# Zero matmuls ahead of the first data, transposes spread between score slots, and fewer, larger visits to attention

The kernel runs on one core of a Trainium2 chip. The metric is the device time of one execution in microseconds (us). Times are medians over several runs. In the traces PE is TensorE, which does the matmuls, DVE the vector engine and ACT the activation engine; PSUM is the memory that matmuls write and the other engines empty ("evacuate"). The *granted clock* is the share of full speed that the trace records for TensorE.

## The reference, cut to what matters

```python
# q, k, v: (8 batches, 12 heads, 448, 64); w_in: (768, 2048); w_out: (2048, 768)
scores = (q @ k.T) / sqrt(64)
attn   = maximum(scores, 0) ** 2 / 448
x      = (attn @ v), heads joined          # 3584 tokens x 768
h      = x @ w_in                          # "m1" below
g      = h * sigmoid(1.702 * h)
out    = g @ w_out                         # "m2" below
```

## The kernel before

A *unit* is four heads of one batch: 3 units a batch, 24 in all. A unit has 7 score *slots* of four 64x64 matmuls, which run in the four quadrants of the array at once. ACT takes the relu of a slot out of PSUM (`rl`), DVE squares it (`at`). After its 7 slots comes attn @ v (`av`, 28 matmuls), which DVE copies into `xt`, the input of m1. Scores and `av` share three PSUM tiles of two banks; m1 (`ht`), m2 (`op`) and the transposes (`tr`) share two tiles of one bank.

```python
def scores(u, j):                      # one slot
    sc = ps_s.tile([128, 2, 512], F32, tag="sc")        # ps_s: 3 buffers
    for s in range(2):
        for a in range(2):
            nc.tensor.matmul(out=sc[c, a, 0:S], lhsT=st["kT"][r, j, c], rhs=st["qT"][r, :, c], ...)

def trans_pe(u, n, cut):               # 14 transposes of q or k, then the copy
    ps = ps_m.tile([128, 1024], F16, tag="mm")           # ps_m: 2 buffers
    ...
    if cut:     nc.scalar.activation(out=t[:, 0:cut, :], in_=ps[:, 0:cut * 128], func=AF.Copy)
    if cut < J: nc.vector.tensor_copy(out=t[:, cut:J, :], in_=ps[:, cut * 128:J * 128])

# (cut)
# first stage: units 0 to 2, attention alone
trans_pe(0, "k", J); trans_pe(0, "q", 4)
while pos[0] < b0:
    visit(1); n += 1
    if n == 4:  trans_pe(1, "k", 0); trans_pe(1, "q", 0); ...   # also at 11 and 19
visit(3)
# second stage: first pass of m1 with units 3 to 5 between
for f in range(NF):
    m1(0, f)
    if f in (2, 8): trans_pe(4 + f // 8, "k", 0); trans_pe(4 + f // 8, "q", 0)
    if f % 2 == 1 or f > 12: visit(min(3, b1 - pos[0]))
prefetch(8, 0)
for m in range(gblk[0] // 2): m2(0, m, 0)
# third stage: m1 and m2 mixed; a visit of three slots whenever enough work has passed
#   (2.6 us at first, 4.2 us later)
```

From unit 6 on q and k are transposed by DMA: loaded, cast on DVE and GpSimd, then transposed. `visit(3)` issues three slots (or two slots and an `av`), and holds back the relu of the third until after the next m1 or m2.

## Time and profile before

| | before |
|---|---|
| time, median of the runs (range) | 407.58 us (407.47 to 409.45) |
| first score matmul | 8.31 us |
| first m1 matmul; its fifth, the first that needs unit 2 | 31.02; 32.15 us |
| first m2 matmul | 64.04 us |
| first visit after it | 77.81 us |
| end of the span in the profile | 406.5 us |

These are starts of instructions in the trace, counted from the span's start. They cut the run into stages. The page, the windows, the chain and the timeline of this kernel are shown in the prediction below. A window's row reads: from:to, length, busy time of PE, weight loads, DVE, ACT, GpSimd, then granted clock, DMA share and GB/s. A timeline row reads: start, length, engine, line, instruction, and in brackets the idle time before it with what ended it.

### The profile page before, as it was taken

Reading aid. Unit: us, or ns where it says so; the run is one execution under the profiler, and the core shown is the slowest. Engines: PE = TensorE matmul, PEld = TensorE weight load, DVE = VectorE, ACT = ScalarE, POOL = GpSimd, SP = SyncE. Lnnn points to the kernel's source line nnn. Section 1 sums busy time; section 2 is a strip of 40 time slices with the busy share of each in tenths; the row PEclk is TensorE's granted clock in tenths of the full one; section 3 lists DMA queues with packets and bytes.
Section 4 is the critical chain, followed back from the end, with each engine's and each line's share of the span. In section 5 each row is a group of like instructions: output and inputs, shape, how many; then the busy total and the mean of one; then the engine's idle time right before and its main releaser. Section 6 shows DMA issues by size and latency. Waiting matters only on the chain.

```text
span 406.5 us, 7792 instructions
## 1 busy us (share of the span) xinstructions
PE 383.3 (94%) x3192; PEld 202.2 (50%) x3192; DVE 190.7 (47%) x294; ACT 205.3 (51%) x297; POOL 130.8 (32%) x200
## 2 busy tenths in 40 slices
PE   3777899899999999999999999999999999999995
PEld 2433455344455455444455555444455555455564
DVE  0894763267746565564466455546354321010121
ACT  4984771576866454556475446546745511322100
POOL 8453424434433143244133324312311222323100
PEclk9989999999999999999999999999999999999999
DMA  8999997589775653955747396845121111111133
GB/s 122 194 204 205 205 290 153 115 192 246 184 173 111 165 139 72 261 106 134 183 70 166 71 198 153 197 51 82 40 52 35 39 40 40 40 39 40 39 79 78
DMA packets 65220, 50.85 MB, mean 125 GB/s; under 512 B 35744, under 2 KB 61728, under 8 KB 65184
## 3 DMA queue, kind: packets, MB, share of 16 engines
q1 hardware_dynamic: 47792, 35.60, 35.5%
q0 software_dynamic: 17152, 14.55, 24.0%
q8 instruction: 25, 0.41, 0.4%
q10 hardware_dynamic: 240, 0.20, 0.2%
q14 instruction: 11, 0.09, 0.1%
HBM read 45.61 MB, written 11.01 MB: 139 GB/s over the span
## 4 chain that ended last, share of the span: by engine, by line
PE 84%; DVE 6%; ACT 5%; issue 2%; DMA 2%; POOL 0%; ACTq 0%; DVEq 0%; POOLq 0%
PE op L278 35%; PE ht L249 33%; PE sc L144 7%; PE av L169 7%; ACT rl L158 4%; DVE at L159 3%; DMA q<-in_q_dram 1%; DVE rl L155 1%; DVE xt L186 1%; DMA qT<-q 1%; ACT gf L254 1%; DVE kT L134 1%; DVE k L101 0%; POOL gt L256 0%; PE tr L127 0%
## 5 line engine op out<-in xcount | busy, mean ns | idle before, releaser
L158 ACT ACTIVATE rl<-sc 128x896 f16<-128x896 f32 x165 | 144.8, 920 | 49.7 <-PE sc L144 49.7
L249 PE MATMUL ht<-xt,win 128*128 128x384 f16 (+1 forms) x768 | 158.4, 353 | 4.4 <-DVE kT L134 3.4
L159 DVE TENSOR_TENSOR at<-rl 128x896 f16<-128x896 f16 x168 | 114.9, 692 | 87.7 <-ACT rl L158 87.4
L256 POOL TENSOR_SCALAR gt<-gf 128x384 f16<-128x384 f32 (+1 forms) x128 | 77.6, 606 | 235.7 <-ACT gf L254 234.7
L278 PE MATMUL op<-wout,gt 128*128 128x384 f16 (+1 forms) x912 | 153.2, 323 | 0.0
L254 ACT ACTIVATE gf<-ht 128x384 f32<-128x384 f32 (+1 forms) x128 | 70.4, 550 | 119.6 <-PE ht L249 106.8
L278 PEld LDWEIGHTS <-gt 128*128 128x128 f16 x912 | 88.0, 98 | 60.5 <-issue 2.7
L249 PEld LDWEIGHTS <-win 128*128 128x128 f16 x768 | 71.1, 98 | 81.6 <-issue 21.4
L284 DVE TENSOR_SCALAR osb<-op 128x384 f32<-128x384 f32 (+1 forms) x57 | 31.3, 549 | 108.0 <-PE op L278 106.5
L144 PE MATMUL sc<-qT,kT 64*64 64x448 f16 x672 | 48.6, 367 | 6.8 <-DVE qT L134 3.0
L169 PE MATMUL av<-at,v 64*64 64x448 f16 x672 | 38.0, 360 | 2.3 <-ACT rl L158 1.4
L144 PEld LDWEIGHTS <-kT 64*64 64x64 f16 x672 | 17.5, 107 | 33.2 <-issue 22.9
L186 DVE CAST xt<-av 128x768 f16<-128x768 f32 (+2 forms) x36 | 26.9, 774 | 8.4 <-PE av L169 8.3
L169 PEld LDWEIGHTS <-v 64*64 64x64 f16 x672 | 20.1, 109 | 16.9 <-issue 7.1
L88 POOL DMA_DIRECT2D v<-in_v_dram x24 | 17.9, 745 | 5.2 <-DMA win<-in_moe_w_in_dram 2.9
L101 POOL CAST q<-qst 128x896 f16<-128x896 f32 x18 | 16.9, 941 | 0.3
L101 DVE CAST k<-kst 128x896 f16<-128x896 f32 x18 | 14.0, 785 | 0.0
L127 PE MATMUL tr<-ident,k 128*64 128x128 f16 x84 | 4.2, 253 | 5.2 <-DMA k<-in_k_dram 5.2
L134 DVE COPY qT<-tr 128x896 f16<-128x896 f16 (+1 forms) x6 | 3.4, 572 | 7.0 <-ACT qT L132 7.0
L127 PEld LDWEIGHTS <-k 128*64 128x64 f16 x84 | 3.1, 128 | 6.9 <-DMA k<-in_k_dram 5.2
L296 POOL DMA_DIRECT2D win<-in_moe_w_in_dram x8 | 5.4, 674 | 2.3 <-DMA q<-in_q_dram 1.3
L116 POOL DMA_DIRECT2D q<-in_q_dram x6 | 4.3, 713 | 3.0 <-PE sc L144 1.3
(17 smaller groups left out, 26.2 us busy)
## 6 DMA issues: line engine op xcount, KB each, us to landing
out_dram<-osb SPq DMA_DIRECT2D x54, 192.0 KB, 2.7
kst<-in_k_dram SPq DMA_DIRECT2D x18, 448.0 KB, 4.9
qst<-in_q_dram SPq DMA_DIRECT2D x18, 448.0 KB, 5.6
v<-in_v_dram POOLq DMA_DIRECT2D x24, 224.0 KB, 4.7
win<-in_moe_w_in_dram POOLq DMA_DIRECT2D x8, 384.0 KB, 11.5
wout<-in_moe_w_out_dram POOLq DMA_DIRECT2D x4, 768.0 KB, 12.1
k<-in_k_dram POOLq DMA_DIRECT2D x6, 224.0 KB, 8.9
q<-in_q_dram POOLq DMA_DIRECT2D x6, 224.0 KB, 8.9
```

The costliest lines, as they stand in the source:

```text
L88: nc.gpsimd.dma_start(out=x, in_=quad(v, b, pr))
L101: eng.tensor_copy(out=o, in_=i)
L144: nc.tensor.matmul(out=sc[c, a, 0:S], lhsT=st["kT"][r, j, c], rhs=st["qT"][r, :, c], start=True, stop=True)
L158: nc.scalar.activation(out=rl, in_=sc[:, :, 0:S], func=AF.Relu)
L159: nc.vector.tensor_tensor(out=at, in0=rl, in1=rl, op=ALU.mult)
L169: nc.tensor.matmul(out=st["av"][64 * a:64 * a + 64, s, 0:S], lhsT=st["v16"][r, a, 64 * j:64 * j + 64], rhs=at[r, a, :], start=(j == 0), st ...
L186: nc.vector.tensor_copy(out=xts[g][:, 2 * pr:2 * pr + 2, 64 * (lo - gcum[g]):64 * (hi - gcum[g])], in_=av[:, :, 64 * (lo - b * J):64 * (hi ...
L249: nc.tensor.matmul(out=ht[:, 0:n], lhsT=w[:, kk, fo:fo + 128], rhs=xts[g][:, kk, 0:n], start=(kk == 0), stop=(kk == NK - 1))
L254: nc.scalar.activation(out=gf[:, 0:n], in_=ht[:, 0:n], func=AF.Gelu_apprx_sigmoid, scale=1.0 / SC)
L256: nc.gpsimd.tensor_scalar(out=gts[g][:, f, 0:n], in0=gf[:, 0:n], scalar1=SC, scalar2=1.0, op0=ALU.mult, op1=ALU.mult)
L278: nc.tensor.matmul(out=op[:, 0:w], lhsT=gts[g][:, f, m * 128:(m + 1) * 128], rhs=wout[h][f // WO][:, f % WO, part * w:(part + 1) * w], sta ...
L284: nc.vector.tensor_scalar(out=ot[:, lo:lo + w], in0=op[:, 0:w], scalar1=1.0 / SC, scalar2=None, op0=ALU.mult)
```

## The change

The intent is to take away waits of TensorE in the first 100 us, and the cost of switching between full-array and quadrant work later. It has five parts.

```diff
+        nc.vector.memset(zero, 0.0)                      # 1: zero matmuls
+        zp = ps_m.tile([128, 512], F32, name="zp", tag="mm")
+        for _ in range(8):
+            nc.tensor.matmul(out=zp, lhsT=zero[:, 0:128], rhs=zero, start=True, stop=True)
...
-        if n == 4: trans_pe(1, "k", 0); trans_pe(1, "q", 0) ...
+        early = {("s", 0, 0): (1, "k"), ("s", 0, 1): (1, "q"), ("s", 1, 0): (2, "k"),   # 2: first stage
+                 ("s", 1, 1): (2, "q"), ("s", 2, 3): (3, "k"), ("s", 2, 5): (3, "q")}
+        # the transpose goes between a slot's matmuls and its relu; its copy is all on DVE
...
-            if f in (2, 8): trans_pe(4 + f // 8, "k", 0); trans_pe(4 + f // 8, "q", 0)
+        trans_at = {0: (4, "k"), 2: (4, "q"), 6: (5, "k"), 8: (5, "q")}                  # 3: m1 pass
...
+        prefetch(9, 7)                                   # 4: earlier prefetch
         for m in range(gblk[0] // 2):
             m2(0, m, 0)
+            if m == 0:
+                prefetch(9, 8)
...
+    for u in range(2 * NP, NU):                          # 5: visits
+        new = [("s", u, j) for j in range(J)]
+        if u > 2 * NP:
+            new.insert((1, 3, 2)[u % 3], ("v", u - 1, 0))
+        rest += new
+        n = 4 if rest[1][0] == "v" else 3                # slot, av, slot, slot - or three slots
...
-                moe.append((x, 4.2))
+                moe.append((x, 4.8))
```

The thresholds follow the number of visits (2.6 to 2.9, 4.2 to 4.8), and `at` gets an eleventh buffer.

More of the change, by code (lines that the diff above doesn't have):

```diff
@@ L52 @@
     rlp = ctx.enter_context(tc.tile_pool(name="rlp", bufs=3))
-    atp = ctx.enter_context(tc.tile_pool(name="atp", bufs=10))
+    atp = ctx.enter_context(tc.tile_pool(name="atp", bufs=11))
     xtp = ctx.enter_context(tc.tile_pool(name="xtp", bufs=3))
@@ L63 @@
     warm = cst.tile([1, 1], F32, name="warm")
+    zero = cst.tile([128, 512], F16, name="zero")
     win = [cst.tile([128, NK, WQ * 128], F16, name=f"win{i}") for i in range(NF // WQ)]
@@ L119, in load16, with trans_pe @@
         st[n + "16"] = x
-    def trans_pe(u, n, cut):
+    def trans_pe(u, n):
         st = units[u]
@@ L130, in trans_pe @@
         t = qkT.tile([128, J, 128], F16, name=f"{n}T", tag=f"{n}T")
-        if cut:
-            nc.scalar.activation(out=t[:, 0:cut, :], in_=ps[:, 0:cut * 128], func=AF.Copy)
-        if cut < J:
-            nc.vector.tensor_copy(out=t[:, cut:J, :], in_=ps[:, cut * 128:J * 128])
+        nc.vector.tensor_copy(out=t, in_=ps[:, 0:J * 128])
         st[n + "T"] = t
@@ L194 @@
     items = []
-    for u in range(NU):
-        late = u > 0 and u != 2 * NP
+    for u in range(2 * NP):
         items += [("s", u, 0), ("s", u, 1)]
-        if late:
+        if u:
             items.append(("v", u - 1, 0))
         items += [("s", u, j) for j in range(2, J)]
-        if u == 2 * NP - 1 or u == NU - 1:
-            items.append(("v", u, 0))
+    items.append(("v", 2 * NP - 1, 0))
+    rest = []
+    for u in range(2 * NP, NU):
[3 more added lines that the diff above has]
+        rest += new
+    visits = []
+    while rest:
+        n = 4 if rest[1][0] == "v" else 3
+        visits.append(rest[:n])
+        rest = rest[n:]
+    visits.append([("v", NU - 1, 0)])
     ats = {}
@@ L236, in visit, with visit4 @@
                 ats[u, j] = relu2(u, j, sc)
+    def visit4(new):
+        release()
+        if len(new) < 4:
+            items[:] = new
+            pos[0] = 0
+            return visit(3)
+        (_, u0, j0), (_, uv, _), (_, u1, j1), (_, u2, j2) = new
+        sc = scores(u0, j0)
+        ats[u0, j0] = relu2(u0, j0, sc)
+        for jj in range(J):
+            av_mm(uv, jj, ats.pop((uv, jj)))
+        sc1 = scores(u1, j1)
+        sc2 = scores(u2, j2)
+        xt_evac(uv)
+        done_units[0] = uv + 1
+        ats[u1, j1] = relu2(u1, j1, sc1)
+        held.append((u2, j2, sc2))
     gts = {}
@@ L344, with slot @@
         w1(1)
-        trans_pe(0, "k", J)
-        trans_pe(0, "q", 4)
+        trans_pe(0, "k")
+        trans_pe(0, "q")
         b0 = items.index(("s", NP, 0))
-        n = 0
-        while pos[0] < b0:
-            visit(1)
-            n += 1
-            if n == 4:
-                trans_pe(1, "k", 0)
-                trans_pe(1, "q", 0)
-                load16(4, "k")
-                load16(4, "q")
-                load_v(4)
-                w1(2)
-            if n == 11:
-                trans_pe(2, "k", 0)
-                trans_pe(2, "q", 0)
-                load16(5, "k")
-                load16(5, "q")
-                load_v(5)
-            if n == 19:
-                trans_pe(3, "k", 0)
-                trans_pe(3, "q", 0)
-                w1(3)
+        def slot(tr=None):
+            t, u, j = items[pos[0]]
+            pos[0] += 1
+            if t == "v":
+                for jj in range(J):
+                    av_mm(u, jj, ats.pop((u, jj)))
+                xt_evac(u)
+                return
+            sc = scores(u, j)
+            if tr:
+                trans_pe(*tr)
+            ats[u, j] = relu2(u, j, sc)
+        early = {("s", 0, 0): (1, "k"), ("s", 0, 1): (1, "q"), ("s", 1, 0): (2, "k"),
+                 ("s", 1, 1): (2, "q"), ("s", 2, 3): (3, "k"), ("s", 2, 5): (3, "q")}
+        loads = {("s", 0, 3): lambda: (load16(4, "k"), load16(4, "q"), load_v(4), w1(2)),
+                 ("s", 1, 3): lambda: (load16(5, "k"), load16(5, "q"), load_v(5)),
+                 ("s", 2, 4): lambda: w1(3)}
+        while pos[0] < b0:
+            it = items[pos[0]]
+            slot(early.get(it))
+            if it in loads:
+                loads[it]()
         visit(3)
-        b1 = items.index(("s", 2 * NP, 0))
+        b1 = len(items)
         pool_work = {1: lambda: w2(0, 0), 2: lambda: w2(0, 1),
                      4: lambda: w2(1, 0), 5: lambda: w2(1, 1)}
+        trans_at = {0: (4, "k"), 2: (4, "q"), 6: (5, "k"), 8: (5, "q")}
         for f in range(NF):
             m1(0, f)
-            if f in (2, 8):
-                trans_pe(4 + f // 8, "k", 0)
-                trans_pe(4 + f // 8, "q", 0)
+            if f in trans_at:
+                trans_pe(*trans_at[f])
             if f in pool_work:
@@ L402, with step_visit @@
         prefetch(8, 0)
+        prefetch(9, 7)
         for m in range(gblk[0] // 2):
             m2(0, m, 0)
-        def step_visit(n):
-            visit(n)
-            if pos[0] < len(items):
-                u = items[pos[0]][1] + (items[pos[0]][0] == "v")
+            if m == 0:
+                prefetch(9, 8)
+        def step_visit():
+            visit4(visits.pop(0))
+            if visits:
+                u = max(x[1] for x in visits[0] if x[0] == "s") if len(visits) > 1 else NU
                 prefetch(u + 4, u + 2)
@@ L416 @@
                                   [("m2", 0, m, 1) for m in range(gblk[0] // 2)])):
-            moe.append((x, 1000.0 if i < 3 else 2.6))
+            moe.append((x, 1000.0 if i < 3 else 2.9))
         for g in range(2, NG + 1):
@@ L421 @@
             for x in mix(a, c):
-                moe.append((x, 4.2))
+                moe.append((x, 4.8))
         for n, (it, tv) in enumerate(moe):
-            if n == 0:
-                prefetch(9, 7)
             if n == 2:
-                prefetch(9, 8)
                 acc = 2.0
@@ L432 @@
                 while done_units[0] < need:
-                    step_visit(3)
+                    step_visit()
                 m1(*it[1:])
@@ L440 @@
                 acc += T2
-            while acc >= tv and pos[0] < len(items):
-                if all(t == "s" or u // NP - 2 < m1_done for t, u, j in items[pos[0]:pos[0] + 3]):
-                    step_visit(3)
+            while acc >= tv and visits:
+                if all(t == "s" or u // NP - 2 < m1_done for t, u, j in visits[0]):
+                    step_visit()
                     acc -= tv
```

## The prediction

> **What bounds the kernel now.** I read the page first: busy times, the 40 slices, the costly groups.
>
> ```profile
> PE 383.3 (94%) x3192; PEld 202.2 (50%) x3192; DVE 190.7 (47%) x294; ACT 205.3 (51%) x297; POOL 130.8 (32%) x200
> ...
> PE   3777899899999999999999999999999999999995
> ...
> DVE  0894763267746565564466455546354321010121
> ACT  4984771576866454556475446546745511322100
> ...
> L158 ACT ACTIVATE rl<-sc 128x896 f16<-128x896 f32 x165 | 144.8, 920 | 49.7 <-PE sc L144 49.7
> ...
> L159 DVE TENSOR_TENSOR at<-rl 128x896 f16<-128x896 f16 x168 | 114.9, 692 | 87.7 <-ACT rl L158 87.4
> ```
>
> TensorE is the bound from about 100 us on; before that its busy share is 7 to 8 tenths while DVE and ACT are at 7 to 9. So a gain can come from the first quarter, or from matmul time that is spent without streaming. I cut the span where the trace changes its pattern (first score at 8.31, first matmul of m1 at 31.02, first of m2 at 64.04) and read the windows:
>
> ```profile
> 8.31:31.02 22.71, 17.69 (x261) 9.24 (x260) 18.75 (x33) 19.47 (x23) 11.83 (x18) 0.92 1.24 198
> 31.02:64.04 33.02, 28.31 (x317) 14.76 (x313) 21.20 (x31) 19.77 (x31) 11.82 (x19) 1.00 1.21 238
> 64.04:98.57 34.53, 32.33 (x251) 15.89 (x250) 16.12 (x26) 20.04 (x28) 16.26 (x22) 1.00 0.78 168
> 98.57:327.00 228.43, 227.77 (x1900) 117.70 (x1897) 123.06 (x185) 129.54 (x188) 69.70 (x103) 1.00 0.56 122
> ```
>
> (columns: length; busy of PE, weight loads, DVE, ACT, POOL; clock; DMA share; GB/s). In the first stretch ACT and DVE are both busy over 80%: attention alone, limited by the evacuation of scores. In the second nothing is full: PE idles 4.7 us in waits. Overlapping matmul records hide more, so I compare starts with what the same groups take undisturbed. The chain of waits gives that:
>
> ```profile
> 101.34 0.69 PE sc L144 x12
> 102.03 2.70 PE ht L249 x12
> ...
> 358.08 2.59 PE ht L249 x12
> ```
>
> Twelve m1 matmuls of 512 columns take 2.59 us at the end of the run, where no attention is mixed in, and 2.70 where scores follow: 0.11 us lost on entering the 64x64 work. Twelve score matmuls, four at a time in quadrants, should stream 3 x 448 columns: at 2.59/12/512 = 0.42 ns a column 0.57 us, but take 0.69: 0.12 lost on the way back. One **visit** to attention costs about 0.23 us beside its work. I count 49 such returns from 31 us on.
>
> Last, the timeline for the single events:
>
> ```profile
> 5.18 0.96 PE L127 MATMUL tr<-ident,k 128*64 128x128 f16 x14 [5.18 <-DMA k<-in_k_dram]
> ...
> 8.31 1.33 PE L144 MATMUL sc<-qT,kT 64*64 64x448 f16 x12 [1.08 <-DVE qT L134]
> ...
> 16.93 0.58 PE L127 MATMUL tr<-ident,k 128*64 128x128 f16 x14
> ...
> 37.71 0.62 DVE L134 COPY kT<-tr 128x896 f16<-128x896 f16 x1
> 38.25 0.62 DVE L134 COPY qT<-tr 128x896 f16<-128x896 f16 x1
> 38.39 1.14 PE L249 MATMUL ht<-xt,win 128*128 128x384 f16 x6 [1.84 <-DVE kT L134]
> ```
>
> The same 14 transposes take 0.96 us at 5 us and 0.58 at 17 us: TensorE starts at half speed. The clock records agree: full speed begins at 13.88 us, and another half-speed stretch lies at 27.54 to 30.95 (the windows' 1.00 before the first record is no measurement). At 38.39 m1 had waited 1.84 us for the copies of a pair of transposes, since both fill the two PSUM buffers that m1 needs; the second pair, at 48, does the same (waits of "PE ht" for "DVE kT": 3.4 us in two).
>
> **The Trainium skill.** "TensorE: Matmul & The Clock Gate", Part 1, says that the array runs at half clock until a free-running window of about 3.4 us was busy. The trace agrees (0.96 against 0.58; the half-speed stretch is 3.41 us). Its Part 4 adds that transposes do not count as busy in the same way; the trace cannot separate this. "TensorEngine Tiling (Array Packing)", section Tiling Modes, Key Properties: changing the tiling mode drains the array. The trace agrees: 0.11 and 0.12 us at the two edges of a visit.
>
> **Part 1, zero matmuls.** Eight of 512 columns, at half clock 2 x 0.216 = 0.43 us each, 3.45 us in all. The vector memset can be done by about 1.3 us, so they end at about 4.8, before the first k lands (5.14). They cost nothing and may bring full clock at 5 to 8 us in place of 13.88. What that buys before the first score: q lands at 6.23, transposes end at 6.85 warm (7.24 cold), and the q copy, now wholly on DVE, takes 0.62: first score 7.5 (warm) or 7.9 (cold) against 8.31; the first relu moves from 8.95 to about 7.95 or 8.6.
>
> **Part 2, transposes between the first 21 slots.** The limit stays. A slot's relu follows the last by 0.81 us on ACT, so seven take 5.7. On DVE a unit is 7 products x 0.57 + 2 copies x 0.54 + its xt copy 1.08 = 6.1 us (spacings in the timeline), and the work is only reordered. Walking DVE's program order by hand: first copy at 8.6 (k of unit 1 lands at 8.06), products of unit 0 done at 14.7 (15.9 before), of unit 2 at about 28.2 (28.9), xt of unit 2 starts at 29.8 (31.14). Gain to the first m1: **1.4 us**, of which 0.6 is the half-clock attn @ v at 28.3.
>
> **Part 3, four single transposes in the first m1 pass**, at f = 0, 2, 6, 8 instead of pairs at 2 and 8. The waits of 1.84 and 1.55 us should shrink but not go: the q copy is behind the products of the visit before it in DVE's order, and the next visit's unit needs it. By hand the first pair gives back 0.45, the second 0.85: **1.3 us**. No load comes late: win lands at 20.3, 27.2, 34.6, 42.3, wout's first half at 49.7, all before their use.
>
> **Part 4, earlier prefetch of units 6 and 7** (ahead of m2 rather than after it). The cast of k is at 72.51 behind the m2 copies, although k landed at 57.5. It can now run at about 61, and q's at 65 (behind the v issues on POOL), so qT lands near 69 and the first visit after m2, at about 74, waits no more: **0.7 us** (0.63 waited now, plus its edge). A later wait at 96 us (0.64 plus 0.38) may go too: **0.4**.
>
> **Part 5, visits.** From unit 6 on, 126 slots and 18 attn @ v: now 144 / 3 = 48 visits; after, 7 for each of 6 batches and one for the last attn @ v = 43. Five visits x 0.23 = **1.2 us**; the thresholds 4.8 and 2.9 keep attention's pace (4.2 x 8/7). The fourth slot needs the PSUM buffer of the first, whose relu ends about 1.5 to 1.6 us after the visit's start, when the slot is due at 1.7: hidden, with little to spare. I charge 0.2 for odd misses. The extra product buffer only makes room.
>
> **Sum:** 1.4 + 1.3 + 0.7 + 0.4 + 1.2 - 0.2 = 4.8 us. After 98 us TensorE has no slack, so what is saved earlier reaches the end. 407.6 - 4.8 = 402.8; as my hand walk of the waits may overstate those that remain, I take **401.8 us**.
>
> **Rivals.** (a) *Evacuation is the bound of the first 31 us, so warm matmuls and spread transposes are hidden.* For it: ACT 19.47 and DVE 18.75 of 22.71 us. Then parts 1 and 2 give 0.5 at most: about 403.5. (b) *The waits go entirely*: pairs 3.4 us, attn @ v tails, cold stretch 2: 8 to 10 us, 398 to 399. For it: PE's ideal streaming in 31 to 64 us is only some 26 of 33 us. Against: DVE's order still puts products ahead of copies. (c) *Loads become the bound*: DMA is busy without a break from 3 to 65 us at about 200 GB/s, and a shift of m2 to 61 leaves 1 us between q's landing (59.8) and its use; a gain above 5 us here would meet it. (d) *The fourth slot waits for its buffer*: 18 visits x 0.5 us = 9 us lost at worst, about 409. Against: relu timing above. (e) *The clock drops again in the thin first stage*, as it did at 27.54: 1 to 1.5 us back.
>
> **Range and chances.** Known gains (visits, transposed pairs, first wait) are 3 us or more, so slower needs rival (d): 3%. Over 2% means below 399.4, 8.2 us: rival (b), 22%. Within 2%: 75%. Range 398.4 to 405.4.
>
> **What would show it.** Full clock before 9 us and a 0.58 us pair of q transposes at 6.3 (part 1); first m1 near 29.5, resumed by 31 (part 2); no PE wait over 1 us for kT or qT before the first m2, which starts near 61 (part 3); no wait for DMA qT after m2 (part 4); 43 returns from attention after unit 5 with 0.23 us each, and no gap before the fourth slot (part 5). I am wrong if the first stage shortens by over 3 us, if PE waits for the fourth slot's relu, or if the clock stays at half after the zero matmuls.

## The result, and the profile after

The changed kernel takes 403.8 us (403.05 to 404.48, 4 runs), against 408.15 us of the kernel before in the four runs known then. The ratio is 0.9889, with a 95% interval of 0.9853 to 0.9925. Ratios here are the mean time of one kernel's runs over that of the other's of the same rounds, so they are not quite the ratios of the medians quoted. It is faster by 1.1%, so "within 2%", as forecast; 403.8 lies in the forecast range.

| in the profiled runs | before | after | gained in the stage |
|---|---|---|---|
| first score | 8.31 | 7.61 | 0.70 |
| fifth matmul of m1 | 32.15 | 32.64 | -1.19 |
| first m2 | 64.04 | 63.09 | 1.44 |
| first visit after it | 77.81 | 76.17 | 0.69 |
| end | 406.47 | 402.58 | 2.25 |

The page of the changed kernel, busy times and slices:

```profile
PE 384.2 (95%) x3200; PEld 202.9 (50%) x3200; DVE 187.7 (47%) x296; ACT 204.8 (51%) x295; POOL 133.7 (33%) x200
...
PE   7678999999999999999999999999999999999995
...
DVE  2886674267655554546446555556444311010121
ACT  3885671576764554665555546566646411322100
```

TensorE's first slices still hold 6 to 8 tenths (the 7 in the first is the zeros), and DVE and ACT still 8: the first stage looks as before. From the fifth slice on TensorE shows only nines up to the last; before, the fifth and the eighth were eights. The windows, cut at the same events:

```profile
7.61:30.77 23.16, 17.08 (x260) 9.14 (x260) 18.35 (x32) 19.08 (x23) 12.53 (x19) 0.85 1.24 197
30.77:63.09 32.32, 28.72 (x316) 14.55 (x313) 21.74 (x33) 20.58 (x32) 12.09 (x19) 1.00 1.23 241
63.09:97.00 33.91, 32.99 (x236) 16.18 (x233) 16.42 (x26) 18.99 (x27) 16.68 (x22) 1.00 0.94 193
97.00:323.10 226.10, 225.33 (x1913) 117.95 (x1913) 118.47 (x184) 131.23 (x188) 71.91 (x103) 1.00 0.57 120
```

The first stage was not shortened: 23.16 us for the 22.71 of before, with a granted clock of 0.85 for 0.92. TensorE's idle time fell from 4.7 to 3.6 us in the second and from 2.2 to 0.9 in the third. The timeline shows what happened in the first stage, and one of the two waits for qT that are left in the second:

```profile
5.22 0.58 PE L127 MATMUL tr<-ident,k 128*64 128x128 f16 x14 [0.41 <-DMA k<-in_k_dram]
...
9.25 0.72 PEld L127 LDWEIGHTS <-q 128*64 128x64 f16 x14 [0.38 <-DMA q<-in_q_dram]
9.25 0.96 PE L127 MATMUL tr<-ident,q 128*64 128x128 f16 x14
...
15.51 0.62 DVE L131 COPY kT<-tr 128x896 f16<-128x896 f16 x1
16.04 0.62 DVE L156 TENSOR_TENSOR at<-rl 128x896 f16<-128x896 f16 x1
...
16.57 0.62 DVE L131 COPY qT<-tr 128x896 f16<-128x896 f16 x1
...
17.11 0.62 DVE L156 TENSOR_TENSOR at<-rl 128x896 f16<-128x896 f16 x1
17.64 1.15 DVE L183 CAST xt<-av 128x768 f16<-128x768 f32 x2
...
18.84 0.76 PE L141 MATMUL sc<-qT,kT 64*64 64x448 f16 x12 [1.86 <-DVE xt L183]
...
21.86 2.83 PE L166 MATMUL av<-at,v 64*64 64x448 f16 x28 [0.43 <-ACT rl L155]
...
39.61 0.38 PE L141 MATMUL sc<-qT,kT 64*64 64x448 f16 x4 [0.79 <-DVE qT L131]
```

The zeros did their work at once: 14 transposes take 0.58 us at 5.22, where they took 0.96. But at 9.25 they take 0.96 again. The clock records of the trace say full speed from 4.72 us, half from 8.13 to 11.55, full, and half once more from 21.79 to 25.20. In the second half-speed stretch `av` of unit 1 takes 2.83 us, where that of unit 0 (at full speed, 15.01) took 1.52. Just ahead of that, TensorE had waited 1.86 us for a PSUM tile: `av` of unit 0 was done at about 16.5, but its copy to `xt` stands in DVE's program order behind two transposes' copies and two products, and starts at 17.64.

A visit with `av` in the third stage, TensorE alone:

```profile
97.00 0.38 PE L141 MATMUL sc<-qT,kT 64*64 64x448 f16 x4
97.22 1.49 PE L166 MATMUL av<-at,v 64*64 64x448 f16 x28
98.54 0.55 PE L141 MATMUL sc<-qT,kT 64*64 64x448 f16 x8
99.02 2.76 PE L275 MATMUL ht<-xt,win 128*128 128x512 f16 x12
```

Read the starts: one slot, `av` 0.22 us later, two slots 1.32 us after that, m1 0.48 us later. The `av` needs 1.32 us for its stream alone (7 x 448 columns at 0.42 ns) and the two slots 0.38, and the rest of the 0.48 is the return to m1: the fourth slot waited for nothing. From the first m2 on the trace has 43 entries into such work, where the kernel before has 49. (The prediction says "49 such returns from 31 us on"; the 49 count from 64 us, and from 31 us there are 57. The price of one is not touched by that slip.)

The waits of TensorE from 64 to 140 us, in the kernel before:

```profile
PE sc L144 <- DMA qT<-q: 1.1, 2, 0.6
PE sc L144 <- ACT rl L158: 1.1, 1, 1.1
PE ht L249 <- DVE osb L284: 0.7, 1, 0.7
```

and in the changed one:

```profile
PE sc L141 <- ACT rl L155: 0.9, 1, 0.9
PE av L166 <- DVE at L156: 0.8, 1, 0.8
```

(waiter, waited for: us in total, times, longest). The waits for transposed q are gone. One wait of `av` for its last product is new, at 106.6 us: that visit came two m1 after the one whose third slot it needs, and DVE did a cast of k first.

### The profile page after: what moved, and what is told of

Same layout as the page of the kernel before. It is cut to its first block, busy times and chain, and to the rows that moved or that the text cites. A ratio compares the mean times of both kernels' runs of the same rounds, so it can differ in the third digit from the quotient of the medians.

```text
span 402.6 us, 7803 instructions
## 1 busy us (share of the span) xinstructions
PE 384.2 (95%) x3200; PEld 202.9 (50%) x3200; DVE 187.7 (47%) x296; ACT 204.8 (51%) x295; POOL 133.7 (33%) x200
## 4 chain that ended last, share of the span: by engine, by line
PE 87%; DVE 5%; ACT 4%; issue 2%; DMA 1%; POOL 0%; ACTq 0%; POOLq 0%
PE op L304 36%; PE ht L275 35%; PE sc L141 8%; PE av L166 7%; ACT rl L155 4%; DVE at L156 2%; DMA q<-in_q_dram 1%; DVE qT L131 1%; PE tr L127 1%; DVE rl L152 1%; ACT gf L280 1%; DVE xt L183 0%; DVE kT L131 0%; DVE k L102 0%; POOL k L117 0%
## 5 line engine op out<-in xcount | busy, mean ns | idle before, releaser
L282 POOL TENSOR_SCALAR gt<-gf 128x384 f16<-128x384 f32 (+1 forms) x128 | 80.1, 626 | 216.5 <-ACT gf L280 215.9
L156 DVE TENSOR_TENSOR at<-rl 128x896 f16<-128x896 f16 x168 | 110.9, 664 | 85.0 <-ACT rl L155 84.7
L141 PEld LDWEIGHTS <-kT 64*64 64x64 f16 x672 | 18.3, 107 | 35.2 <-issue 22.7
L131 DVE COPY kT<-tr 128x896 f16<-128x896 f16 x6 | 3.7, 621 | 6.9 <-PE tr L127 6.9
L117 POOL DMA_DIRECT2D k<-in_k_dram x6 | 4.5, 757 | 2.2 <-DMA v<-in_v_dram 1.4
L358 PE MATMUL zp<-zero 128*128 128x512 f16 x8 | 3.6, 628 | 1.2 <-DVE zero L355 1.2
```

The source lines that it names most:

```text
L156: nc.vector.tensor_tensor(out=at, in0=rl, in1=rl, op=ALU.mult)
L282: nc.gpsimd.tensor_scalar(out=gts[g][:, f, 0:n], in0=gf[:, 0:n], scalar1=SC, scalar2=1.0, op0=ALU.mult, op1=ALU.mult)
```

## The experiments

The theory after reading both traces was: parts 3, 4 and 5 gain what the table shows; in the first stage the evacuation limits, the spread transposes cost time there, and the early clock is lost again. The rival: the early clock is worth all its half-speed time, and spreading helps wherever it is done. Twelve kernels were run, five rounds each. Kernels of one group share the runs of the kernel before, whose times go from 407.4 to 410.1 us. All results were correct.

### Each part alone, put into the kernel before

**zeros_only** (part 1):

```diff
+        nc.vector.memset(zero, 0.0)
+        for _ in range(8): nc.tensor.matmul(out=zp, lhsT=zero[:, 0:128], rhs=zero, ...)
```

> The kernel before plus the eight zero matmuls and nothing else. Theory (the first stage is limited by evacuation, and the clock falls back to half when TensorE is thinly used): first score 0.3 to 0.8 us earlier, the first m1 moves by less than 0.8 us, the total by -0.3 us (-1.0 to +0.5). Rival (full clock from 5 us on is worth what the half-speed matmuls had lost, all of it on the path): first m1 1.2 us or more earlier, total -1.2 to -2.

Ratio 0.998 (0.9954 to 1.0005), that is -0.8 us, median 407.22. First score at 7.88 in place of 8.31. The fifth m1 matmul came at 30.61, 1.54 us earlier, which in this profile speaks for the rival; the time lies at the edge of the theory's range (-1.0 to +0.5) and short of the rival's. The profiles differ in the clock as well, which is taken up below.

**spread_first_only** (part 2, with all copies on DVE):

```diff
-        visit(1) ... if n == 4: trans_pe(1, "k", 0); trans_pe(1, "q", 0)
+        slot(early.get(it))                  # the slot's own transpose, if it has one
```

> The kernel before with only the transposes of the first 21 slots spread (and all their copies on DVE). Theory (DVE does the same work in another order, and two copies now stand ahead of the xt copy that frees the PSUM buffer): first score 0.3 us earlier, one wait of PE for xt of 1 to 2 us in unit 1, total +0.5 us (-0.3 to +1.3). Rival (spreading takes waits off the path): total -1 us or better.

Ratio 1.0043 (1.0015 to 1.0071): +1.7 us, median 410.2. The rival is out: this part costs time. TensorE's longer waits in the first 34 us, here:

```profile
PE sc L140 <- DVE qT L130: 2.3, 2, 1.5
PE sc L140 <- ACT rl L154: 2.2, 5, 0.6
PE sc L140 <- DVE xt L182: 2.1, 2, 1.9
```

In the kernel before the third kind is small:

```profile
PE sc L144 <- DVE xt L186: 0.8, 2, 0.4
```

So the wait of nearly 1.9 us for `xt` comes with this part alone. First score 7.96, fifth m1 matmul 33.27.

**spread_m1_only** (part 3):

```diff
-    if f in (2, 8): trans_pe(4 + f // 8, "k", 0); trans_pe(4 + f // 8, "q", 0)
+    if f in trans_at: trans_pe(*trans_at[f], 0)
```

> The kernel before with only the four transposes of the first m1 pass taken one at a time (f = 0, 2, 6, 8). Theory: the two waits of m1 for kT (1.84 and 1.55 us) go, two waits of scores for qT of 0.5 to 0.9 us take their place, total -1.4 us (-0.8 to -2). Rival (the stage is limited by DVE, so the waits only change name): total within 0.5 us.

Ratio 0.9958 (0.9935 to 0.9981): -1.7 us, median 406.46. The waits of m1 for kT are gone from the list of 31 to 64 us, and this stands in their place:

```profile
PE sc L144 <- DVE qT L134: 1.4, 2, 0.8
```

From the fifth m1 matmul to the first m2 the stage takes 30.46 us in place of 31.89. That is the theory's number.

**prefetch_only** (part 4):

```diff
+        prefetch(9, 7)
         for m in range(gblk[0] // 2):
             m2(0, m, 0)
+            if m == 0: prefetch(9, 8)
-            if n == 0: prefetch(9, 7)        # in the third stage
-            if n == 2: prefetch(9, 8)
```

> The kernel before with only the prefetch of units 6 and 7 taken ahead of m2. Theory: the wait of 0.63 us for DMA qT at the first visit after m2 goes, and of the waits between 93 and 98 us (1.0 us together) some stay because their loads are issued by the visits as before: total -0.8 us (-0.4 to -1.6). Rival (the gain at these waits in the changed kernel comes from the new grouping of visits, or the waits move on): total within 0.3 us.

Ratio 0.9993 (0.9964 to 1.0021): -0.3 us, and the interval holds both expectations, so the time decides nothing. The trace does: from first m2 to the first visit 13.07 us in place of 13.77, while the later wait for qT stays.

**visits_only** (part 5):

```diff
-                    step_visit(3)            # thresholds 2.6, 4.2
+                    step_visit()             # 3 slots, or slot, av, slot, slot; thresholds 2.9, 4.8
```

> The kernel before with only the new grouping of visits (43 in place of 48 after unit 5, four slots where attn @ v is among them). Theory (an entry to and return from the 64x64 work costs 0.23 us, and the fourth slot finds its buffer free): total -1.3 us (-0.8 to -2.2 if a wait such as the one of 0.92 us at 131 us goes too), gaps before fourth slots under 0.1 us. Rival (the fourth slot waits for the relu of the first, which eats it): total within 0.4 us or slower, with waits of scores for rl after each attn @ v.

Ratio 0.9949 (0.993 to 0.9969): -2.1 us, median 406.18. Entries fall from 49 to 43. The largest loss at a fourth slot's edge is that one wait of `av` for its last product (0.93 us at 106 us); no slot waits for the relu of its visit's first. The two waits between 93 and 98 us and the one of 0.83 us at 131 us are gone too, so part of the gain that the prediction gave to part 4 belongs here. (This run also has the eleventh `at` buffer. Its share was not measured apart; no wait list of the kernel before names a wait for such a buffer.)

Added up, the five parts give -0.8 + 1.7 - 1.7 - 0.3 - 2.1 = -3.2 us. Measured together: 0.9889, -4.5 us. Each of the six numbers has an interval of about 1 us either way, so the sum does not contradict the whole, but it proves no more than the order of the parts. The profiles are sharper. From the fifth m1 matmul on, the stages of all profiles with the same code there agree within 0.3 us, mostly within 0.1: 31.9 us to the first m2 without part 3 and 30.5 with it, 13.8 to the first visit without part 4 and 13.1 with it, 328.6 to 328.8 from there to the end without part 5 and 326.4 to 326.7 with it. So the three give 1.4, 0.7 and 2.3 us, 4.4 together, and what else differs between these profiles lies before the fifth m1 matmul, which comes anywhere from 30.6 to 33.3 us.

### The price of a visit

**two_slot_visits**: two slots a visit, thresholds at two thirds.

```diff
-                moe.append((x, 4.2))
+                moe.append((x, 2.8))
-                    step_visit(3)
+                    step_visit(2)
```

> The kernel before with two slots a visit after unit 5 in place of three, at two thirds of the threshold: 72 visits for 48. It prices the edges of a visit. Theory: each further entry costs 0.23 us, so with 20 to 24 more entries in the trace total +4.6 to +5.5 us, beside new waits that the trace names. Rival (the drain at the edges is hidden under the weight loads and only looks like time): under +2 us.

Ratio 1.0157 (1.0133 to 1.0181): +6.4 us. The trace has 71 entries for 49. In its profile the first m2 starts 1.08 us late, with two half-speed stretches in the first stage that have nothing to do with the edit. From there to the end it lost 5.6 us over 22 entries: 0.25 us each, small waits included. Its chain of waits in the third stage:

```profile
200.16 2.69 PE ht L249 x12
202.85 0.50 PE sc L144 x8
203.35 2.71 PE op L278 x16
```

Two slots stream in 0.38 us (2 x 448 columns at 0.42 ns) and take 0.50; twelve m1 matmuls take 2.69 for 2.59, sixteen of m2 2.71 for 2.60. The edges cost what the prediction read from the kernel before: the rival is out.

### The first stage: order, zeros and clock

**after_no_zeros** (the changed kernel without part 1):

```diff
-        for _ in range(8): nc.tensor.matmul(out=zp, lhsT=zero[:, 0:128], rhs=zero, ...)
```

> The changed kernel without its zero matmuls. Theory: the same as or up to 1 us slower than the changed kernel (ratio to before 0.989 to 0.992), since the first stage is limited by evacuation and the clock drops twice in the changed kernel. Rival: 1.5 us slower or more (0.993 and up).

Ratio 0.9928 (0.9906 to 0.9949), median 404.93. It stands between the two expectations: the zeros are worth 0.8 us alone and about 1.6 here (0.9928 against 0.9889), with intervals that overlap.

**after_twice** (each score matmul of the first 21 slots issued twice into the same place):

```diff
-        for s in range(2):
+        for s in [0, 1] * (2 if u < NP else 1):
```

> The changed kernel with each score matmul of the first 21 slots issued twice into the same place (the second overwrites the first with the same values; the result is right). It doubles a cost of TensorE there and keeps the array busier. Theory (TensorE is not the limit there, and the clock's fall to half, which cost attn @ v 1.24 us and its followers, comes from too little work): no half-speed stretch between 8 us and the first m1, first m1 1 to 2 us earlier than in the changed kernel in spite of 21 x 0.19 = 4 us more matmul work, total -1 us against the changed kernel (ratio to before about 0.986). Rival (TensorE's own time is on the path there): 1 to 4 us slower than the changed kernel.

Ratio 0.9895 (0.9875 to 0.9914), median 403.75. Neither number came out. Four us more of matmul work in the first stage made no difference that can be measured. That speaks against TensorE as the limit there, but does not prove it: the edit also kept the clock up, and a cost and a gain may have cancelled. The hoped-for gain of 1 us is not in the times either, although in the profiled run the clock stayed full from 5.03 us on and the fifth m1 matmul came 1.14 us earlier than in the changed kernel.

**after_late** (transposes of unit 2 at slots 3 and 5 of unit 1):

```diff
-("s", 1, 0): (2, "k"), ("s", 1, 1): (2, "q")
+("s", 1, 3): (2, "k"), ("s", 1, 5): (2, "q")
```

> The changed kernel with the transposes of unit 2 at slots 3 and 5 of unit 1 (as it does for unit 3 in unit 2) in place of slots 0 and 1, so that the xt copy of unit 0 no longer stands behind both copies and two products in DVE's order. Theory (that order made TensorE wait 1.86 us for xt, and it is why spreading in the first stage costs time): this wait falls under 1.0 us and the total by 0.8 us against the changed kernel (0.3 to 1.3), ratio to before 0.987. Rival (DVE's sum of work limits the stage, in any order): within 0.3 us of the changed kernel.

Ratio 0.9892 (0.9861 to 0.9923): no different from the changed kernel. TensorE's waits, up to 330 us:

```profile
PE sc L141 <- DVE qT L131: 4.7, 5, 1.4
...
PE sc L141 <- DVE xt L183: 1.2, 2, 0.8
```

The wait for `xt` fell to 0.8 us as the theory said, but the later copies of q now hold up the next unit's scores instead (up to 1.4 us). The wait was moved, and the mean time is the rival's case. But the clock is in that mean too. The result of each timed run lists its mean granted clock (one half-speed window of 3.41 us lowers it by 0.004, and so can the idle end of a run): the two runs at 1.000 took 402.2 and 402.3 us, the four at 0.987 to 0.989 took 404.2 to 405.6. What this order is worth at full clock stays open.

**after_first_as_before** (the changed kernel with the first stage as it was, zeros kept):

```diff
-        slot(early.get(it))
+        visit(1) ... if n == 4: trans_pe(1, "k", 0); trans_pe(1, "q", 0)
```

> The changed kernel with the first stage as it was (pairs of transposes, unit 0's copies on ACT and DVE), the zero matmuls kept. Theory (the first-stage spread is the one part that costs): the four other parts alone add up to -0.8 - 1.7 - 0.3 - 2.1 = -4.9 us, ratio to before 0.988, so 0 to 1 us faster than the changed kernel. Rival (with the zero matmuls the spread pays): 0.7 us or more slower than the changed kernel, ratio 0.991 and up.

Ratio 0.9859 (0.9835 to 0.9884), median 402.55: 1.2 us faster than the changed kernel (0.9859 against 0.9889), though the two intervals overlap. It agrees with spread_first_only, whose interval lies wholly above 1: part 2 costs time, 1.7 us there and 1.2 here. A surprise is in this run's timeline:

```profile
1.22 3.60 PE L362 MATMUL zp<-zero 128*128 128x512 f16 x8 [1.22 <-DVE zero L359]
5.16 0.95 PE L128 MATMUL tr<-ident,k 128*64 128x128 f16 x14 [0.35 <-DMA k<-in_k_dram]
```

against zeros_only, where the code is the same up to here:

```profile
1.22 3.59 PE L333 MATMUL zp<-zero 128*128 128x512 f16 x8 [1.22 <-DVE zero L330]
5.13 0.58 PE L128 MATMUL tr<-ident,k 128*64 128x128 f16 x14 [0.32 <-DMA k<-in_k_dram]
```

The same zeros brought full clock in one execution and not in the other. To see why, I took the 14 profiles, cut the first 32 us of each into the windows of 3.413 us that their clock records mark, and took the share of each window in which a matmul record (transposes included) is open:

| what the clock did at the window's end | windows | busy share of the window |
|---|---|---|
| half to full | 23 | 0.86 to 1.00 |
| stayed half | 21 | 0.00 to 0.86 |
| full to half | 10 | 0.44 to 0.62 |
| stayed full | 61 | 0.52 to 0.92 |

So in these profiles full clock came after one window that was at least 0.86 busy. The fall has no such edge: all 6 windows at full clock that were at most 0.50 busy were followed by half speed, but of the 21 that were 0.52 to 0.62 busy only 4 were, and none above. The window's phase is not the kernel's: the first boundary lies 0.2 to 3.2 us after the span's start, differently in each profile. Eight zeros last 3.6 us. In after_first_as_before the boundaries were at 2.99 and 6.40; that window held the end of the zeros, a gap and the transposes, was just 0.86 busy, and the clock stayed at half until 13.23. In the changed kernel the boundaries were at 1.31 and 4.72, and the zeros filled the window. And a first stage that is limited by evacuation keeps TensorE at 0.45 to 0.9 a window, near the level at which the clock falls. That is an association over 14 profiles, not an experiment on the threshold itself; after_twice, which raised the share, is the one deliberate test: it lost the clock in none of its windows, and its six timed runs have a mean clock of 0.996 to 1.000 where the changed kernel's four have 0.989 to 1.000.

With that the first stages can be sorted (us from first score to fifth m1 matmul):

| kernel | order of the first stage | half speed after the first score | length |
|---|---|---|---|
| zeros_only | pairs | 8.13 to 11.54 | 22.72 |
| prefetch_only | pairs | to 13.11 | 22.98 |
| visits_only | pairs | to 12.46 | 23.05 |
| after_first_as_before | pairs | to 13.23 | 23.09 |
| after_best3 (below) | pairs | to 13.44 | 23.09 |
| before | pairs | to 13.88, 27.54 to 30.95 | 23.83 |
| spread_m1_only | pairs | to 17.64 | 24.09 |
| two_slot_visits | pairs | to 11.58, 15.00 to 18.41, 28.65 to 32.06 | 24.96 |
| after_twice | spread, doubled scores | none | 23.80 |
| after_best2 (below) | spread, late | none | 23.10 |
| after_late | spread, late | to 11.07, 14.48 to 17.90 | 24.81 |
| after | spread | 8.13 to 11.55, 21.79 to 25.20 | 25.03 |
| after_no_zeros | spread | to 12.46, 22.70 to 26.12 | 25.18 |
| spread_first_only | spread | to 11.90, 22.14 to 25.56 | 25.31 |

after_late and after_best2 have the same code in this stage: 1.7 us apart. Their clocks differ and their code does not. That is why one profile of the first stage decides little: the pairs go from 22.7 to 25.0 us, the spread orders from 23.1 to 25.3. All three profiles of the plain spread order with single scores (after, spread_first_only, after_no_zeros) fell to half speed at 21.8 to 22.7 us, after a window 0.45 to 0.50 busy: the one with the wait of 1.86 us for `xt`. So in these profiles the order costs twice: its wait, and the half-speed `av` that follows.

### Versions that beat both

**after_best2**: after_late with two waits of the changed kernel's trace taken out.

```diff
-            if f % 2 == 1 or f > 12:
+            if f % 2 == 1 and f < 15:        # last av: now after the first third of m2
-                acc = 2.0
+                acc = 1.5                    # second visit after m2 one m1 later
```

> after_late with two more waits of the changed kernel's trace taken out: the last attn @ v of the first m1 pass goes behind the first third of m2 (its 1.27 us wait for the last product goes), and the second visit after m2 comes one m1 later (its 1.39 us wait for a relu goes). Theory (TensorE has no slack from there on, so each wait taken out is gained at the end): 2.2 us less than after_late (1.5 to 2.7), ratio to before 0.982. Rival (the waits reappear at the next buffer): under 0.8 us less than after_late.

Ratio 0.9818 (0.9791 to 0.9844), median 401.38: 3 us less than after_late, more than the 2.2 expected. The clock fits the rest: from the fifth m1 matmul to the end the profiles differ by 2.15 us, and the runs at a mean clock of 1.000 took 399.8 and 400.3 us for after_late's 402.2 and 402.3. Neither wait is left in the trace; one of 0.2 us for DMA qT is new.

**after_best3**: the same two edits on after_first_as_before.

> The changed kernel with the first stage as before (as in the earlier run of that) and the two further waits taken out (last attn @ v of the first m1 pass behind the first third of m2, second visit after m2 one m1 later). Theory (the two corrections are independent: 0.9859 for the first alone, and the other two took 0.0074 off where they were added): ratio to before 0.978 to 0.981. Rival (the waits that after_best2 removed were only open because its first stage came late, so that the loads were there): 0.983 or more, with a wait for DMA qT after m2.

Ratio 0.9817 (0.9795 to 0.984), median 400.79 (400.05 to 401.56): between the two expectations; no wait for DMA qT, so the rival's reason is not there. Against after_first_as_before (0.9859) the two waits brought 1.7 us (2.4 in the profiles, from the fifth m1 matmul to the end). The two best versions cannot be told apart; both are 1.8% faster than the kernel before and 0.7% faster than the changed one.

## Why the prediction was right

The forecast of 401.8 us lay 2 us below the 403.8 measured, and within its range. Part of that is luck: the first stage was forecast to gain 1.4 us and lost 0.5 in the profiles, while the stage of the visits, for which 0.4 + 1.2 - 0.2 = 1.4 us stood, gained 2.25. By its own steps:

- **Parts 1 and 2, 1.4 us: mis-sized, and of the wrong sign for part 2.** In the profiles the fifth m1 matmul moved from 32.15 to 32.64, half a us later; the prediction's sign for part 2, first m1 near 29.5 and resumed by 31, came at 30.77 and 32.64. The first score came at 7.61, as the "warm" case said (7.5). What failed is the hand walk of DVE's order. "The limit stays", it says, a relu each 0.81 us, and so it had the products of unit 0 done at 14.7 and those of unit 2 at 28.2. They were done at 15.6 and 29.9. The relus before, and after:

```profile
8.95 3.35 ACT L158 ACTIVATE rl<-sc 128x896 f16<-128x896 f32 x4 [1.08 <-PE sc L144]
...
8.04 0.92 ACT L155 ACTIVATE rl<-sc 128x896 f16<-128x896 f32 x1 [5.81 <-PE sc L141]
9.37 0.92 ACT L155 ACTIVATE rl<-sc 128x896 f16<-128x896 f32 x1 [0.41 <-PE sc L141]
10.78 5.77 ACT L155 ACTIVATE rl<-sc 128x896 f16<-128x896 f32 x7 [0.49 <-PE sc L141]
```

  The first gaps became 1.33 and 1.41 us, since on TensorE a transpose that waits for its load (0.38 us at 9.25) and runs at half speed (0.96) now stands ahead of the next slot's matmuls. With full clock there, in after_best2, they were 0.93 and 1.18, so order and clock both have a part. The wait of 1.86 us for `xt`, which the prediction does not mention, and the half-speed `av` came on top. Rival (e), "the clock drops again in the thin first stage", put at 1 to 1.5 us, is what came, twice. Rival (a), that the evacuation hides these parts, is supported by after_twice but not proved. Measured alone, the zeros bring 0.8 us (an interval that just holds zero) and the spreading costs 1.7.
- **Part 3, 1.3 us: right.** 1.44 us in the trace, 1.7 (0.8 to 2.6) alone. The waits changed their name to qT and shrank from 1.84 and 1.55 us to 0.8 and less, as told.
- **Part 4, 0.7 us: right in the trace** (0.69), though its time alone (-0.3) does not stand clear of noise. The further 0.4 us credited to it came, but from the new visits.
- **Part 5, 1.2 us: right in mechanism, under-sized.** 2.1 us alone. Six entries fewer at 0.23 give 1.4, and the waits that go with the old grouping (0.8 us at 93 to 98 and 0.83 at 131, without their edges), less the new one of 0.94, give 0.7 more: 2.1. The prediction's 0.64 plus 0.38 at 96 us counts the edges of that visit in. two_slot_visits measured the price at 0.25, small waits included.
- **The sum, 4.8 us,** was nearer to the 4.5 measured than the 5.8 that the forecast took from it. The step from 402.8 to 401.8, "my hand walk of the waits may overstate those that remain", went the wrong way in the first stage.
- Rival (c), loads as the bound, and rival (d), the fourth slot, did not show: no wait for DMA after m2, and no gap at fourth slots.

What stays open: how much of the first stage's loss is order and how much clock in the timed runs. Their clock is recorded as a mean but not controlled. Three runs of prefetch_only at a mean clock of 1.000 took 406.8 to 407.5 us, the other three, at 0.992, took 408.7 to 408.8; and not every kernel splits so (the slowest run of the changed one, 404.48, has 1.000).

## What to carry to other kernels

Count how often TensorE switches between quadrant and full-array work, and take the price from the trace: here 0.23 us a round trip, so 6 fewer were worth more than any reordering of the first stage that was tried. When transposes or other extra work are spread over a stage limited by DVE, look at what they now stand in front of in TensorE's and in DVE's program order, a copy that frees a PSUM buffer above all. And before believing a change in a stage that uses TensorE thinly, compare the clock records of the two profiles, and the lengths of the stages that the change did not touch.

## What the Trainium skill lacked or had wrong

- "TensorE: Matmul & The Clock Gate", Part 1, gives the free-running window and, as its abstract rule, no idle gaps over about 3.4 us. The runs show that no such gap is needed: the clock fell after windows of 3.413 us that were still 0.44 to 0.62 busy (10 of 10 falls), with no idle stretch longer than 1.86 us. The same Part tells, as a second failure mode, of a clock that swings with short idle times, but gives no busy share. Here the clock rose only after windows at least 0.86 busy (23 of 23 rises). As the window's phase is free, 3.6 us of matmuls in a row are not always enough: two of the seven profiles with zeros kept half clock past 13 us. Split evenly over two windows it would take 2 x 0.86 x 3.413 = 5.9 us, an estimate from these numbers.
- The same page, Part 4, says that full clock does not engage for transposes and that they do not count as busy in the same way. Here 11 of the windows before a rise were 0.40 to 0.58 busy without their transposes and 0.86 to 1.00 with them (before, 10.47 to 13.88, among others), while one 0.56 busy without and 0.64 with them stayed half (spread_m1_only, 7.40 to 10.81). Transposes also run at full clock once it is there, 0.58 against 0.96 us for 14.
- "TensorEngine Tiling (Array Packing)", Tiling Modes, says that changing the mode drains the array, with no figure. The runs show 0.11 us at the entry and 0.12 at the return for 64x64 against 128x128, 0.25 us a visit with small waits.
